# Block 0 of an attention-and-FFN kernel by halves of the heads, with four d_ff tiles begun early

## The chip, the cores and the metric

The kernel runs on 1 core of one Trainium2 chip. The metric is the device time of one execution in microseconds (us), lower is better. Its engines are TensorE (PE, with its weight loads shown apart as PEld), VectorE (DVE), ScalarE (ACT), GpSimd (POOL) and SyncE (SP), which here does nothing but issue transfers. Each engine works through its own instructions in order; semaphores tie them together.

## The reference, cut to what matters

```python
# q, k, v: (8, 8, 576, 64); w_in: (512, 2048); w_out: (2048, 512)
scores = 1/sqrt(64) * q_c @ k_c.T        # within chunks of 64 positions
attn = softmax(scores)
out = attn @ v_c                         # (8, 8, 576, 64)
x = out.transpose(0, 2, 1, 3).reshape(4608, 512)
h = maximum(x @ w_in, 0)
y = h*h @ w_out                          # (4608, 512), float32
```

Attention is local to chunks of 64 positions. Its result, with the 8 heads side by side in 512 columns, goes through a feed-forward network (FFN) with a squared ReLU.

## The kernel before, in words

**Tiling.** The 4608 tokens are 18 groups of 256, and two groups are a block of 512 tokens, so there are nine blocks. For each group the kernel loads q, k and v in fp32 and takes the upper halves of their words as bf16 (the index `1::2` after a bitcast). q and k are transposed so that the head's 64 elements lie on the partitions (`transpose_qk`, lines 414 to 428; from group 4 on by a cast on POOL and a transposing transfer on SP, `cast_q`, `cast_k`, `transpose_qk_dma`, lines 446 to 462). `scores` (464) makes all scores of a group in one PSUM bank pair of 128x1024 and ACT takes their exponential into `e`. `values` (496) multiplies by V, whose tiles hold a column of ones behind each head's 64, so that the sum of the exponentials comes out as column 65; `out_of_x` (438) takes its reciprocal on DVE (line 442) and multiplies (line 443) into `x`. `transpose_x` (530) or, in block 0, `transpose_x_early` (517) turns x into xT, the right operand of the FFN. `ffn_in` (573) makes h in 16 tiles of 128 d_ff rows (ft 0 to 15), each from four matmuls (dt 0 to 3, 128 of the 512 columns of x each: two heads each); ACT does the ReLU (590) and DVE or ACT the square (596, 598) into gT. `ffn_out_by_ft` (895) makes the output of block 0; blocks 1 to 8 use forms with fewer products (`ffn_out`, 728, and the quads from line 652 on).

**Heads and chunks.** On the 128 partitions lie two chunks. For the odd heads the chunks of a pair are swapped, so V of the even heads is kept in tiles `ve_sb` (two per group) and V of the odd heads in tiles `vo_sb` that start half a tile (64 positions) earlier; five `vo_sb` tiles serve the two groups of a block, the first and the last of them half full.

**Block 0 (lines 967 to 991).** The two groups follow each other. SP issues, in this order: q and k of group 0, q and k of group 1 (512 KB each, in runs of 512 B), nine V loads (128 KB or 64 KB each, in runs of 256 B), then the eight w_in loads (512 KB each, all 512 rows of 256 columns, runs of 1 KB). The first w_in load is cast half by POOL and half by ACT (lines 330 to 335). On PE stand: the transposes of q and k of group 0, of q of group 1, the scores of group 0, the transposes of k of group 1, then values, scores and x transposes of both groups, with `keep_busy` (430) matmuls of no use in the places where PE would wait. `ffn_in` of block 0 begins with ft 0 and 1 for the 256 tokens of group 0, then for those of group 1, then the other 14 tiles for all 512 tokens.

**What sets the order.** The order on each engine is that of the program (`manual_schedule`, line 205). From block 0's FFN on, a plan by slots places the attention of later blocks between FFN steps (lines 1004 to 1077): a slot is one step of `ffn_in` or `ffn_out`. In the plan of block 0 (`j == 0`) one load of group 4 or 5 (block 2) is issued in each of the first slots: first q and k, then V. In the plan of block 1 (`j == 1`) the casts of groups 4 and 5 stand in slots 16 and 20, their transposing transfers in slots 21 and 25, their scores in slots 36 and 37, and their values in 38 and 40. From its ninth load on SP waits, before it issues a load, for the landing of the one eight loads earlier: eight semaphores go round.

Of the kernel before, what the change touches and what calls it, by code (L numbers as in the profile page):

```python
# [144 lines left out]
def kernel(  # L145
# [9 lines left out]
    nc = tc.nc  # L155
# [83 lines left out]
    n_rec = itertools.count()  # L239
    v_even = [w_pool.tile([128, 2, n_hp, D + 1], FP32, name=f"ve_sb{i}") for i in range(NV)]  # L240
    v_odd = [w_pool.tile([128, n_hp, D + 1], FP32, name=f"vo_sb{i}") for i in range(NO)]
    for vt in v_even:
# [61 lines left out]
    def v_pieces(g):  # L304

        even, odd = [], []
        for t, p, m, b, s in runs(g):
            even.append(lambda t=t, p=p, m=m, b=b, s=s: nc.sync.dma_start(  # L308
                out=v_even[g % NV][p:p + m, t, :, 0:D],
                in_=v[b, 0::2, s:s + m, :].rearrange("h s d -> s h d")))  # L310
        for n, p, m, b, s in odd_loads[g]:
            odd.append(lambda n=n, p=p, m=m, b=b, s=s: nc.sync.dma_start(  # L312
                out=v_odd[n % NO][p:p + m, :, 0:D],
                in_=v[b, 1::2, s:s + m, :].rearrange("h s d -> s h d")))
        if g < 2:
            yield from [even[0], *odd[:-1], even[1], odd[-1]]
        else:
            yield from even + odd

    def go(pieces):  # L320
        for f in pieces:
            f()
# [3 lines left out]
    def load_w_in(i, n_cast=1):  # L326
# [4 lines left out]
        for c in range(0, 256, n):  # L331
            if i == 0 and c:
                return lambda: nc.scalar.copy(out=w_in_bf[:, :, c:c + n], in_=st[:, :, c:c + n])
            nc.gpsimd.tensor_copy(  # L334
                out=w_in_bf[:, :, i * 256 + c:i * 256 + c + n], in_=st[:, :, c:c + n])
# [180 lines left out]

    def transpose_x_early(g, t):
        psb = ps_ffn.tile([128, 512], FP32, name="ps_ffn").bitcast(BF16)
        x = state["x", g]
        for hp in range(n_hp):  # L520
            nc.tensor.transpose(
                out=psb[:, hp * 128:(hp + 1) * 128],
                in_=x[:, t, hp].rearrange("p a d -> p (a d)"),
                identity=ident)
        copy = nc.vector.tensor_copy if t and g else nc.scalar.copy
        copy(
            out=x_tile(g // 2)[:, g % 2 * 2 + t].rearrange("p h q -> p (h q)"),
            in_=psb[:, 0:512])

# [41 lines left out]
    FT_ORDER = [*range(n_ft // 2, n_ft), *range(n_ft // 2)]  # L571

    def ffn_in(j, parts):
        gT = gT_main.rearrange("p (u h) (f t) -> p u h f t", u=2, f=4)
        xT = xTs[j]
        for u, (c, n, ft) in enumerate((c, n, ft) for c, n, fts in parts for ft in fts):
            h = ps_ffn.tile([128, 512], FP32, name="ps_ffn")
            for dt in range(n_dt):
# [4 lines left out]
                    start=(dt == 0), stop=(dt == n_dt - 1))  # L583
            if n == 512 or u % 2 == 0:
                state["rl"] = state.get("rl", -1) + 1
                rl_tile = relu_sb[state["rl"] % 4]
                if j < 3:
                    rl_tile = rl_tile.bitcast(BF16)
            rl = rl_tile[:, u % 2 * 512:] if n < 512 else rl_tile
            nc.scalar.activation(out=rl[:, 0:n], in_=h[:, 0:n], func=AF.Relu)  # L590
            u0, u1 = c // GT, (c + n) // GT
            dst = gT[:, u0:u1, ft // 4, ft % 4, :]
            src = rl[:, 0:n].rearrange("p (u t) -> p u t", t=GT)
            if (n == 512 and ft in SQUARES_ON_ACT) or (
                    n < 512 and ft in (12, 3)) or (j == 0 and u == 0):
                nc.scalar.activation(out=dst, in_=src, func=AF.Square)
            else:
                nc.vector.tensor_tensor(out=dst, in0=src, in1=src, op=ALU.mult)  # L598
            yield

# [376 lines left out]
    keep_busy(6)  # L977
    AV(0, [1])
    transpose_x_early(0, 0)
    keep_busy(10)  # L980
    transpose_x_early(0, 1)
    AV(1, [0])
    AV(1, [1])
    keep_busy(4)
    transpose_x_early(1, 0)
    cast_first()
    keep_busy(8)
    transpose_x_early(1, 1)
    first_ffn_in = ffn_in(0, [(0, HT, (0, 1)), (HT, HT, (0, 1)), (0, BT, range(2, n_ft))])
    next(first_ffn_in)  # L990
    next(first_ffn_in)

    for i in range(1, 8):
        load_w_in(i, n_cast=2 if i < 5 else 1)
# [9 lines left out]
    for j in range(QUADS):  # L1004
# [6 lines left out]
        if j == 0:  # L1011
            loads, go_slots = pieces(far), range(17)
            at(28, summed(b11_p_b21, b11, b21))
# [6 lines left out]
        elif j == 1:  # L1020
# [201 lines left out]
```

## Time and profile before

| | us |
|---|---|
| median of 3 runs | 277.83 (276.78 to 278.43) |
| the profiled execution, its own time | 276.91 |
| its span from the first to the last instruction | 275.1 |
| PE busy in it | 264.9 (96%) |
| DVE, ACT, POOL busy | 199.2, 168.3, 89.6 |
| PE's first matmul of the FFN | starts at 17.46 |
| granted TensorE clock | 1.0 throughout |

Times in the profile are us from the start of the span. A timeline row gives start and length of a run of like instructions, engine, line, what is written from what, shape, count, and in brackets how long the engine sat idle before and what released it. The chain of waits is followed back from the last instruction. A view of stretches gives the busy time of each engine in each stretch, the granted clock, the mean busy share of the 16 DMA engines and the GB/s moved. "Landing" is the time from issue until all of a transfer's data has arrived.

### The profile page before, as it was taken

The page shows a single profiled execution, that of the slowest core. Times are in us where ns is not written, and L with a number is a line of the kernel's source. Part 1 is how long each engine was busy: PE and PEld are TensorE (multiplying, and loading weights), DVE is VectorE, ACT ScalarE, POOL GpSimd, SP SyncE. Part 2 cuts the span into 40 slices and gives each one's busy share as a digit, 9 for nine tenths or more (in the row PEclk, how much of TensorE's full clock was granted, in tenths as well). Part 3 has the DMA queues.
Part 4 walks back from the last instruction along what each step waited for, and adds up shares of the span by engine and source line. Part 5 has one row for each costly group of instructions (what it writes and reads, how often), then busy time and mean ns, then how long its engine had stood idle before and what let it go on. Part 6 is the DMA issues. An engine that isn't in the chain of part 4 may idle for free.

```text
span 275.1 us, 7923 instructions
## 1 busy us (share of the span) xinstructions
PE 264.9 (96%) x3261; PEld 203.4 (74%) x3261; DVE 199.2 (72%) x365; ACT 168.3 (61%) x300; POOL 89.6 (33%) x122
## 2 busy tenths in 40 slices
PE   2999999999999999999999999999999999999995
PEld 2764445888774588447878888888888888888884
DVE  1457514999538592499989998799779877994752
ACT  1657614894458883877678765565746665756430
POOL 2048834240360012040245224551643212331600
PEclk9999999999999999999999999999999999999999
DMA  7999999999999999999999999697999530220223
GB/s 216 262 352 389 361 332 270 339 213 172 262 210 218 238 234 218 275 223 178 228 236 197 218 238 194 103 220 196 244 187 224 123 76 2 99 55 7 71 83 114
DMA packets 136056, 55.60 MB, mean 202 GB/s; under 512 B 104273, under 2 KB 131921, under 8 KB 136017
## 3 DMA queue, kind: packets, MB, share of 16 engines
q1 hardware_dynamic: 133248, 46.54, 74.0%
q0 software_dynamic: 2624, 8.39, 9.6%
q8 instruction: 26, 0.43, 0.6%
q10 hardware_dynamic: 144, 0.13, 0.1%
q14 instruction: 14, 0.11, 0.1%
HBM read 36.70 MB, written 9.44 MB: 168 GB/s over the span
## 4 chain that ended last, share of the span: by engine, by line
PE 87%; DMA 4%; SPq 3%; DVE 3%; ACT 1%; issue 1%; ACTq 0%; DVEq 0%
PE ps_ffn L657 22%; PE ps_out L780 22%; PE ps_ffn L579 17%; PE ps_ffn L780 14%; PE ps_ffn L901 5%; PE ps_att L510 3%; PE ps_att L540 2%; DMA vo_sb<-in_v_dram 2%; PE ps_att L483 2%; DMA xT<-x 2%; DVE gT L598 2%; SPq L266 1%; SPq L308 1%; SPq L312 1%; DVE x L443 1%; ACT e L494 1%
## 5 line engine op out<-in xcount | busy, mean ns | idle before, releaser
L579 PE MATMUL ps_ffn<-xT,w_in_bf 128*128 128x512 bf16 (+1 forms) x328 | 57.8, 333 | 0.0
L780 PEld LDWEIGHTS <-w_st 128*128 128x128 bf16 x512 | 48.9, 98 | 6.6 <-DVE w_st L614 0.5
L665 DVE CUSTOM_DVE_ANT_0 relu<-ps_ffn,w_st 128x512 f32<-128x512 f32 x60 | 39.3, 684 | 13.0 <-PE ps_ffn L657 11.6
L579 PEld LDWEIGHTS <-w_in_bf 128*128 128x128 bf16 x328 | 31.2, 98 | 21.6 <-POOL w_in_bf L334 0.2
L598 DVE TENSOR_TENSOR gT<-relu 128x256 bf16<-128x256 bf16 (+2 forms) x68 | 34.1, 537 | 17.8 <-ACT relu L590 17.3
L590 ACT ACTIVATE relu<-ps_ffn 128x256 bf16<-128x256 f32 (+2 forms) x82 | 39.4, 501 | 9.4 <-PE ps_ffn L579 8.6
L657 PE MATMUL ps_ffn<-qk_st,w_in_bf 128*128 128x256 bf16 x240 | 35.3, 273 | 0.1
L657 PEld LDWEIGHTS <-w_in_bf 128*128 128x128 bf16 x320 | 30.7, 98 | 4.1 <-issue 0.3
L809 POOL DMA_DIRECT2D out_dram<-o_sb x24 | 17.6, 733 | 43.6 <-DVE o_sb L614 23.3
L780 PEld LDWEIGHTS <-gT 128*128 128x128 bf16 x296 | 28.6, 98 | 3.3
L780 PE MATMUL ps_out<-w_out_bf,w_st 128*128 128x256 bf16 x240 | 30.8, 273 | 0.0
L699 ACT ACTIVATE w_st<-ps_ffn 128x512 f32<-128x512 f32 x20 | 11.9, 597 | 29.6 <-PE ps_ffn L657 29.6
L443 DVE TENSOR_TENSOR x<-ps_att,recs 128x512 bf16<-128x512 f32 x36 | 24.9, 692 | 1.2
L657 PEld LDWEIGHTS <-qk_st 128*128 128x128 bf16 x240 | 22.6, 98 | 3.2 <-DVE qk_st L614 0.3
L657 PE MATMUL ps_ffn<-xT,qk_st 128*128 128x256 bf16 x160 | 23.9, 273 | 0.0
L676 POOL TENSOR_TENSOR qk_st<-relu 128x512 bf16<-128x512 f32 x10 | 10.3, 1034 | 41.6 <-DVE relu L665 38.1
L494 ACT ACTIVATE e<-ps_att 128x1024 bf16<-128x1024 f32 x18 | 18.3, 1025 | 8.5 <-PE ps_att L483 8.5
L676 POOL TENSOR_TENSOR gT<-relu 128x512 bf16<-128x512 f32 x10 | 10.3, 1033 | 35.4 <-DVE relu L665 30.5
L449 POOL CAST qkb<-qk_st 128x1024 bf16<-128x1024 f32 x12 | 13.0, 1082 | 14.9 <-DMA qk_st<-in_q_dram 14.9
L674 ACT ACTIVATE gT<-relu 128x512 bf16<-128x512 f32 x28 | 17.7, 631 | 0.0
L780 PE MATMUL ps_ffn<-w_out_bf,w_st 128*128 128x256 bf16 x144 | 17.7, 273 | 0.0
L614 DVE TENSOR_TENSOR w_st<-gT,w_st 128x1024 bf16<-128x1024 bf16 x26 | 16.8, 682 | 0.0
(92 smaller groups left out, 428.7 us busy)
## 6 DMA issues: line engine op xcount, KB each, us to landing
qk_st<-in_q_dram SPq DMA_DIRECT2D x16, 512.0 KB, 5.6
out_dram<-o_sb POOLq DMA_DIRECT2D x28, 256.0 KB, 3.9
qk_st<-in_k_dram SPq DMA_DIRECT2D x24, 256.0 KB, 5.6
ve_sb<-in_v_dram SPq DMA_DIRECT2D x32, 128.0 KB, 3.9
w_st<-in_moe_w_in_dram SPq DMA_DIRECT2D x8, 512.0 KB, 5.9
w_st<-in_moe_w_out_dram SPq DMA_DIRECT2D x8, 512.0 KB, 5.5
vo_sb<-in_v_dram SPq DMA_DIRECT2D x24, 128.0 KB, 3.6
qk_st<-in_k_dram SPq DMA_DIRECT2D x4, 512.0 KB, 5.8
```

Source lines behind the costliest of these rows:

```text
L443: nc.vector.tensor_tensor(out=x, in0=o[:, :, :, 0:D], in1=rec.to_broadcast([128, 2, n, D]), op=ALU.mult)
L494: nc.scalar.activation(out=e_out, in_=s_in, func=AF.Exp, scale=scale)
L579: nc.tensor.matmul(out=h[:, 0:n], lhsT=w_in_bf[:, dt, ft * 128:(ft + 1) * 128], rhs=xT[:, c // 128:(c + n) // 128, dt, :], start=(dt == 0) ...
L590: nc.scalar.activation(out=rl[:, 0:n], in_=h[:, 0:n], func=AF.Relu)
L598: nc.vector.tensor_tensor(out=dst, in0=src, in1=src, op=ALU.mult)
L614: nc.vector.tensor_tensor(out=out, in0=in0, in1=in1, op=op)
L657: nc.tensor.matmul(out=bank[:, f * GT:(f + 1) * GT], lhsT=a[:, dt, ft * 128:(ft + 1) * 128], rhs=b[:, :, dt, :], start=(first and f == 0 a ...
L665: nc.vector._custom_dve(TENSOR_ADD_SAT, out=out, in0=in0, in1=in1, s0=BIG, s1=0.0)
L674: engine.activation(out=dst, in_=r, func=AF.Square)
L676: engine.tensor_tensor(out=dst, in0=r, in1=r, op=ALU.mult)
L780: nc.tensor.matmul(out=out_ps, lhsT=lhsT, rhs=b[:, i, :], start=(first and i == 0 and (last or t == 0)), stop=(i == HF - 1), skip_group_ch ...
L809: dma.dma_start(out=out[t0:t0 + GT, col:col + HD].rearrange("(t p) d -> p t d", p=128), in_=o_sb.rearrange("p (t d) -> p t d", d=HD))
```

## The change

Block 0 is no longer worked group by group but by halves of the heads: heads 0 to 3 for all 512 tokens, then heads 4 to 7.

- Loads: q and k of a half are 512 KB each as before, now in runs of 1 KB (four rows of a head). V comes by single heads: for each half two loads of 128 KB (even heads) and two of 96 KB (odd heads) and two edges of 32 KB. To take them in one transfer, V tiles of block 0 lie in one tile (`ve_first`, `vo_mid`), which later blocks use in turn as before. w_in for ft 0 to 3 comes in four loads of 256 KB, by halves of the rows: dt 0 and 1 behind q and k of the second half, dt 2 and 3 behind V of the second half. SP's order: q, k, 6 V loads; q, k, 2 w_in, 6 V loads; 2 w_in; then w_in 2 to 7. All four are cast by POOL, none by ACT.
- Transposes of q and k: per half 16 matmuls each, and two copies out of each PSUM bank, one per pair of heads. q's two go to DVE; of k's, the first goes to ACT and the second to DVE. In the built program the DVE copy of k waits for the ACT copy of the same bank.
- Four d_ff tiles (ft 0 to 3, 512 tokens) are begun as soon as their operands exist: dt 0 and 1 (heads 0 to 3) around the scores and values of the second half, dt 2 after the x transposes of heads 4 and 5, dt 3 after those of heads 6 and 7. They stay open in four PSUM banks meanwhile. The squares of ft 0 to 3 all go to DVE in block 0.
- Fillers: 8 before the first scores, 8 after them, 4 before the last x transposes.
- Block 2: V of groups 4 and 5 is no longer issued in the plan of block 0; it is issued in the plan of block 1, slots 18 and 22, and the transposing transfers of q and k move to slots 16 and 20, right behind the casts. So on SP each group's transposing transfer stands ahead of its V loads, where before both stood behind all V loads.

```diff
+    v_first = w_pool.tile([128, 4, n_hp, D + 1], FP32, name="ve_first")
+    v_mid = w_pool.tile([128, 3, n_hp, D + 1], FP32, name="vo_mid")
...
+    def load_w_in_half(r):
+        st = w_st[next(n_staged) % 5].rearrange("p (a f) -> p a f", a=2)
+        for c in (0, 256):
+            nc.sync.dma_start(
+                out=st[:, :, c:c + 256],
+                in_=moe_w_in[256 * r:256 * r + 256, c:c + 256].rearrange("(a p) f -> p a f", p=128))
+            nc.gpsimd.tensor_copy(
+                out=w_in_bf[:, 2 * r:2 * r + 2, c:c + 256], in_=st[:, :, c:c + 256])
...
+        for hp in range(NH):
+            copy = nc.vector.tensor_copy if hp or not which else nc.scalar.copy
+            copy(out=qkT[:, which, hp].rearrange("c (p i) -> c p i", i=4),
+                 in_=psb[:, hp].rearrange("c i p -> c p i"))
...
+    def first_tile(ft, dts):
+        if dts[0] == 0:
+            first_h.append(ps_ffn.tile([128, 512], FP32, name="ps_ffn"))
+        for dt in dts:
+            nc.tensor.matmul(
+                out=first_h[ft],
+                lhsT=w_in_bf[:, dt, ft * 128:(ft + 1) * 128],
+                rhs=xTs[0][:, :, dt, :],
+                start=(dt == 0), stop=(dt == n_dt - 1), skip_group_check=True)
+
+    def first_in():
+        for ft in range(4):
+            first_tile(ft, (3,))
+            squared(0, ft, first_h[ft], 0, BT, ft)
+            yield
+        yield from ffn_in(0, [(0, BT, range(4, n_ft))])
...
-    HT = BT // 2
-    go(pieces([0, 1]))
-    cast_first = load_w_in(0, n_cast=2)
-    TE(0)
-    transpose_qk(1, ps_ffn, None)
-    SC(0)
-    transpose_qk(1, None, ps_ffn)
-    keep_busy(8)
-    AV(0, [0])
-    SC(1)
...
+    act = nc.scalar.copy
+    for half in range(2):
+        qk_half, v_half = half_loads(half)
+        go(qk_half)
+        if half:
+            load_w_in_half(0)
+        go(v_half)
+    load_w_in_half(1)
+    transpose_half(0, 0, ffn_bank())
+    transpose_half(0, 1, ffn_bank())
+    keep_busy(8)
+    scores_half(0)
     keep_busy(8)
-    transpose_x_early(1, 1)
...
+    values_half(0, 0)
+    values_half(0, 1)
+    transpose_half(1, 0, ffn_bank())
+    transpose_x_half(0, 0, ffn_bank(), act)
+    transpose_x_half(0, 1, ffn_bank(), act)
+    transpose_half(1, 1, ffn_bank())
+    scores_half(1)
+    first_tile(0, (0, 1))
+    first_tile(1, (0, 1))
+    values_half(1, 0)
+    first_tile(2, (0, 1))
+    values_half(1, 1)
+    first_tile(3, (0, 1))
+    both = att_bank()
+    transpose_x_half(1, 0, both[:, 0:256], act)
+    for ft in range(4):
+        first_tile(ft, (2,))
+    both = att_bank()
+    fill(4, both[:, 256:384])
+    transpose_x_half(1, 1, both[:, 0:256], nc.vector.tensor_copy)
+    first_ffn_in = first_in()
...
-            loads, go_slots = pieces(far), range(17)
+            loads, go_slots = itertools.chain(*map(qk_pieces, far)), range(17)
...
-                for slot, f in ((16 + 4 * i, C), (21 + 4 * i, TD), (36 + i, SC), (38 + 2 * i, AV),
+                for slot, f in ((16 + 4 * i, C), (16 + 4 * i, TD), (36 + i, SC), (38 + 2 * i, AV),
                                 (41 + 2 * i, XT)):
                     at(slot, f, g)
+                at(18 + 4 * i, lambda g=g: go(v_pieces(g)))
```

`transpose_half`, `scores_half`, `values_half` and `transpose_x_half` do for half of the heads and 512 tokens what `transpose_qk`, `scores`, `values` and `transpose_x_early` do for all heads and 256 tokens; each has as many matmuls and as large a result as the old one.

More of the change, by code (lines that the diff above doesn't have):

```diff
@@ L526, in transpose_x_early, with fill @@
[L526 to L528 removed]
+        copy(out=x_tile(0)[:, :, NH * half + hp, :], in_=psb.rearrange("p (t q) -> p t q", t=4))
+    def fill(n, out):
+        for _ in range(n):
+            nc.tensor.matmul(out=out, lhsT=ident, rhs=ident, start=True, stop=True)
     def transpose_x(g):
```

156 lines of the change are left out of this document (111 added, 45 removed).

## The prediction

> **What bounds the kernel now.** I read the busy totals and slices of the page first, then PE's waits, then the chain of waits, then the timeline of the first 32 us.
>
> ```profile
> PE 264.9 (96%) x3261; PEld 203.4 (74%) x3261; DVE 199.2 (72%) x365; ACT 168.3 (61%) x300; POOL 89.6 (33%) x122
> ...
> PE   2999999999999999999999999999999999999995
> ```
>
> ```profile
> PE ps_ffn L400 <- DMA qk_st<-in_q_dram: 5.2, 2, 4.8
> PE ps_ffn L400 <- DMA qk_st<-in_k_dram: 0.4, 1, 0.4
> PE ps_ffn L657 <- DVE qk_st L614: 0.2, 1, 0.2
> ```
>
> ```profile
> 10.73 4.93 DMA vo_sb<-in_v_dram
> 17.46 14.01 PE ps_ffn L579 x72
> 31.47 7.77 PE ps_ffn L901 x36
> ```
>
> PE is busy for 264.9 of 275.1 us, and its one long wait is the 4.8 us for the first q. After that it is the bound. So what happens ahead of 31.47, the end of block 0's first FFN stage, moves the end of the kernel by as much; what happens beside PE later moves nothing unless PE has to wait. A matmul of 512 columns takes 7.77/36 = 0.216 us. The stage's own work, 56 of these and 16 of half the width, is 64 x 0.216 = 13.8 of its 14.01 us. Ahead of it the chain names the last V load, issued at 10.73 and landed 4.93 later, at 15.66.
>
> ```profile
> 4.77 1.06 PE L400 MATMUL ps_ffn<-ident,qk_st 128*64 128x128 bf16 x16 [4.77 <-DMA qk_st<-in_q_dram]
> 6.26 1.06 PE L400 MATMUL ps_ffn<-ident,qk_st 128*64 128x128 bf16 x16 [0.42 <-DMA qk_st<-in_k_dram]
> 7.37 1.07 ACT L409 COPY qkT<-ps_ffn 128x512 bf16<-128x512 bf16 x2 [5.34 <-PE ps_ffn L400]
> 8.74 0.64 PE L483 MATMUL ps_att<-qkT 64*64 64x64 bf16 x32
> 8.86 1.29 DVE L409 COPY qkT<-ps_ffn 128x512 bf16<-128x512 bf16 x2 [1.69 <-PE ps_ffn L400]
> 9.44 1.02 ACT L494 ACTIVATE e<-ps_att 128x1024 bf16<-128x1024 f32 x1 [1.00 <-PE ps_att L483]
> 10.36 1.03 PE L433 MATMUL ps_ffn<-ident 128*128 128x128 bf16 x8
> 12.83 0.22 PE L510 MATMUL ps_att<-ve_sb,e 64*64 64x65 bf16 x2 [0.19 <-DVE x L443]
> 13.23 0.21 DVE L442 RECIPROCAL recs<-ps_att 128x8 f32<-128x8 f32 x1 [0.46 <-PE ps_att L510]
> 13.48 0.69 DVE L443 TENSOR_TENSOR x<-ps_att,recs 128x512 bf16<-128x512 f32 x1
> 14.22 0.40 PE L521 MATMUL ps_ffn<-ident,x 128*128 128x128 bf16 x4 [0.18 <-DVE x L443]
> 14.66 0.58 ACT L526 COPY xT<-ps_ffn 128x512 bf16<-128x512 bf16 x1 [0.55 <-PE ps_ffn L521]
> 16.43 0.61 PE L433 MATMUL ps_ffn<-ident 128*128 128x128 bf16 x8
> 16.79 0.61 POOL L334 CAST w_in_bf<-w_st 128x512 bf16<-128x512 f32 x1 [14.59 <-DMA w_st<-in_moe_w_in_dram]
> 17.48 0.42 DVE L526 COPY xT<-ps_ffn 128x512 bf16<-128x512 bf16 x1 [0.49 <-PE ps_ffn L521]
> 18.11 1.17 POOL L334 CAST w_in_bf<-w_st 128x512 bf16<-128x512 f32 x2 [0.70 <-DMA w_st<-in_moe_w_in_dram]
> 19.46 2.67 POOL L334 CAST w_in_bf<-w_st 128x512 bf16<-128x512 f32 x4 [0.18 <-DMA w_st<-in_moe_w_in_dram]
> ```
>
> These rows are the price list: a k load waited for to the first copy 1.11 (6.26 to 7.37); a copy out of PSUM 0.535 on ACT, 0.645 on DVE; scores to exponential 0.70 (8.74 to 9.44), exponential 1.02; values to reciprocal 0.40, to product 0.65, product 0.69; x transposes to copy 0.44, that copy 0.58 on ACT, 0.42 on DVE. An engine starts about 0.05 after what released it.
>
> **The change part by part.** *Loads.* The order changes, the bytes up to dt 2 and 3 of ft 0 to 3 do not: 2 MB of q and k, 1 MB of V, 1 MB of w_in, which before had landed at 18.11.
>
> ```profile
> 3.00:9.25 6.25, 3.63 (x80) 2.98 (x80) 1.68 (x3) 1.07 (x2) 0.00 (x0) 1.00 1.16 341
> 9.25:14.00 4.75, 4.56 (x120) 3.66 (x108) 2.52 (x6) 3.60 (x5) 0.00 (x0) 1.00 1.33 227
> 14.00:27.00 13.00, 12.41 (x110) 7.10 (x110) 8.50 (x16) 8.73 (x18) 8.41 (x12) 1.00 1.07 373
> ```
>
> In the last column q and k in runs of 512 B move at 341 GB/s, V in runs of 256 B at 227, w_in in runs of 1 KB at 373. A q or k load took 1.49 us (4.77 to 6.26), a w_in load 1.32 and 1.35 (16.79, 18.11, 19.46), so runs of 1 KB should save q and k 0.14 each, bounded by nothing and 0.17. The first k then lands at 5.98, and the last early weights at 18.11 - 4 x 0.14 = 17.55, cast by 18.16. V's loads of 64 and 128 KB overlapped at 227 GB/s, 0.58 us per 128 KB, so I count the new ones by bytes too; the other end is the second rival below. [...]
>
> *Attention.* Per half there is the same number of matmuls, so the question is latency. From the first k at 5.98: ACT's copy starts 7.09 and ends 7.63; DVE's copy of the same bank waits for it and ends 8.33; the second half of the scores runs at 8.38 and the exponential from 8.8 to 9.82. Values at 9.87, reciprocal 10.3 (0.40, and I take 0.43 while PE is slow), x of heads 0, 1 ready 11.25, of heads 2, 3 at 12.2, since DVE makes them one behind the other. Then x transposes, ACT's copies to 13.27; PE reaches the second k at 12.5, behind the x transposes: its bytes end at 5.98 + 2.3 for half of V + 2 x 1.35 = 11.0, at 12.8 with all of V's old lag (first rival), and I take 12. ACT copies its first part from 13.32 to 13.86, DVE the second to 14.55 (DVE's q copies, 1.29, end at 13.5 and stay hidden). Scores, exponential 14.95 to 15.97, values 16.02, x of heads 4, 5 ready 17.35, its transposes 17.40, ACT's copy to 18.42. Four dt 2 matmuls, 0.86, to 19.33; the 4 fillers, at most 0.3, to 19.55; x of heads 6, 7 is ready since 18.3 but stands behind these; transposes, DVE's copy to 20.41, dt 3 at 20.46.
>
> *FFN.* Left from there are 4 + 48 matmuls: 52 x 0.216 = 11.22, so the stage ends at 31.68 and not at 31.47: **0.2 us later**. The 12 matmuls moved ahead lie in waits and cost nothing, but they save only 2.6 us, while the half-by-half chain has two exponentials and four x products one behind the other and starts its last matmuls 3 us later than the old stage began. The weights (18.16) and the last V (17.55 less a w_in load of 1.33, so 16.2, needed at 16.9) are hidden by 0.3 and 0.7 us: if transfers are later by more than that, they are next. The removed ACT cast and ACT square, and the square moved to DVE, cost nothing:
>
> ```profile
> 22.92 5.16 DVE L598 TENSOR_TENSOR gT<-relu 128x512 bf16<-128x512 bf16 x6 [1.26 <-ACT relu L590]
> ```
>
> a square is 0.86 on DVE, a tile on PE 4 x 0.216 = 0.86, so DVE keeps pace, and 14 of them from 21.7 end at 33.8, when the output stage still uses the first tiles. Were that cover gone, one square is 0.86.
>
> *Block 2.* Here only slack is bought.
>
> ```profile
> 61.66 6.17 SPq L460 DMA_TRANSPOSE qkT<-qkb  x2
> ...
> 68.80 0.45 PE L483 MATMUL ps_att<-qkT 64*64 64x64 bf16 x32
> ...
> 70.15 0.44 PE L483 MATMUL ps_att<-qkT 64*64 64x64 bf16 x32
> ...
> 73.93 0.22 PE L510 MATMUL ps_att<-ve_sb,e 64*64 64x65 bf16 x2
> ```
>
> ```profile
> DMA to landing us min/median/max: 4.9/5.5/6.2
> ```
>
> ```profile
> 58.86 1.17 POOL L454 CAST qkb<-qk_st 128x1024 bf16<-128x1024 f32 x1 [1.61 <-DMA qk_st<-in_k_dram]
> ```
>
> The second transposing transfer, issued about 64.75, lands 4.9 later at 69.7; its scores run at 70.15 without a wait, 0.45 us of slack. After, it waits on SP for the cast that ends at 60.03 and behind group 4's five V loads, about 61.8, and lands some 3 us earlier; behind it on SP stand group 5's V, out by about 67 and, by the same 4.9, landed by 72, needed at 73.93. So 0; without it only a gain in block 0 beyond 0.45 us would be lost here. If V came 3 us later than I say, PE would wait 1 us.
>
> *Sum.* 276.91 + 0.2 = 277.1 against the profiled execution, which lies 0.92 below the median of 277.83; against that median 278.0.
>
> **Rivals.** *Transfers set the end, as before, and they come early (faster).* V's 1 MB at 227 GB/s should end 4.6 us after 9.25, at 13.9; it landed at 15.66. If that lag of 1.8 us does not come back, early weights are cast at 16.4 and V is there at 14.4. By transfers alone dt 2 would then end at 17.3 and, with fillers, transposes and the last copy, dt 3 start at 18.4: the stage ends at 29.6, 1.85 us earlier, 276.0. That takes a copy chain 2 us shorter than mine. For it: PE's share of the chain is priced partly at its slow early pace, and may rise sooner. Against it: the copies, exponentials and products on the chain are DVE's and ACT's, whose durations the rows fix.
>
> *Loads in flight are too few (slower).* From the ninth load on each waits for the landing of the eighth before it, and now 20 loads stand up to the early weights where 15 stood.
>
> ```profile
> DMA to landing us min/median/max: 5.1/5.8/9.4
> ```
>
> This is the w_in and w_out loads' landing. Eight per 5.8 us is 0.73 each: load 8 at about 8.4 (5.98 and half of V) plus 12 x 0.73 = 17.2, no loss against 17.55. At 7.6, midway to the 9.4 seen, it is 0.95 each: 19.8, cast 20.4, dt 2 to 20.9, fillers, last x copy, dt 3 at 22.1: 1.6 us beyond my sum, so 279.6. It begins to cost from about 6.2 us per landing.
>
> *PE falls back to its slow pace in the waits.* Eight fillers took 1.03 us at 10.36 and 0.61 at 16.43: PE is slow at first, though the granted clock reads 1.00 throughout. If the waits between 14.9 and 20.4 bring this back, and it lasts from 8.74 to about 11.5 again, 2.8 us run at half pace: 1.4 us, so 279.4. Against it: waits of 0.5 to 1.5 us in 12 to 17 did not do so. [...]
>
> *It does not do what it says:* the first tiles wait for each other and the 12 early matmuls run in the end anyway: 2.6 us less hidden, 280.6.
>
> **How the numbers follow.** My forecast (276.9 to 279.0 from the 1 KB bound, the start-up pace and the difference of two medians) gets 0.68; the faster rival 0.16, of which I put 0.11 beyond 0.5%, since a chain shortened by half as much gives 277; few in flight 0.09, slow pace 0.04, no overlap 0.03. 0.5% is 1.4 us, about what a measurement of this kernel tells from no change. So faster 0.12 (0.11 and a tail of the forecast), slower 0.14 (the last three less a little), same 0.74. The range takes in most of the faster rival and the slow pace: 276.2 to 279.4.
>
> **What would show it.** In the profile after: FFN matmuls without a break from about 20.5, ending about 31.7; DVE copies of k behind ACT's; the last fillers ahead of the last x transposes although x is ready; casts of early weights done by 18.2; the scores of group 5 with no wait. Wrong if the unbroken FFN starts before 19.3 or after 21.6, or if PE waits for V, a cast or a transposing transfer.

## The result, and the profile after

The kernel after takes **279.78 us** in the median of 22 runs (277.99 to 282.93), the kernel before 278.09 in 22 runs beside it (276.78 to 280.04). The ratio of their runs is **1.0068**, with a 95% interval of 1.0047 to 1.0088: about 1.9 us slower (1.3 to 2.4). The forecast was 278.0 with a range of 276.2 to 279.4, no change beyond 0.5%; it was too low, and the time lies just above its range.

The profiled execution of after took 282.04 us (span 280.2), near the slow end of its own spread, so what is seen only there has to be told from what every execution shows. First the page: busy time, the PE and DMA rows of the 40 slices, and the first two rows on the chain that ended last.

```profile
PE 263.7 (94%) x3234; PEld 200.8 (72%) x3237; DVE 202.3 (72%) x367; ACT 165.8 (59%) x293; POOL 92.0 (33%) x123
...
PE   3779999999899899999999999999999999999994
...
PE 66%; DMA 15%; DVE 8%; SPq 6%; ACT 2%; issue 2%; POOL 1%; DVEq 0%; ACTq 0%; POOLq 0%
PE ps_ffn L781 18%; PE ps_out L904 18%; PE ps_ffn L904 11%; PE ps_ffn L699 8%; DMA qkT<-qkb 7%; PE ps_ffn L1025 5%; DVE gT L692 4%; DMA qk_st<-in_k_dram 4%; DMA vo_sb<-in_v_dram 2%; PE ps_att L509 2%; DMA w_st<-in_moe_w_in_dram 2%; SPq L459
```

PE is as busy as before in us and stands more: the last work is now followed back through transfers for 15% of the span (4% in before), and the transposing transfers of q and k (qkT<-qkb) alone have 7%. The waits of PE, in the view of waits, say where (us in total, times, longest):

```profile
PE ps_att L482 <- DMA qkT<-qkb: 2.6, 3, 1.3
...
PE ps_ffn L622 <- DVE x L442: 0.7, 2, 0.4
PE ps_att L588 <- ACT qkT L575: 0.7, 1, 0.7
PE ps_ffn L713 <- ACT xT L626: 0.7, 1, 0.7
...
PE ps_ffn L713 <- DVE xT L626: 0.5, 1, 0.5
PE ps_ffn L713 <- POOL w_in_bf L556: 0.5, 1, 0.5
```

Now block 0 of after in the timeline of PE, from the scores of the second half on:

```profile
13.88 0.32 PE L588 MATMUL ps_att<-qkT 64*64 64x64 bf16 x16 [0.68 <-ACT qkT L575]
14.60 0.32 PE L588 MATMUL ps_att<-qkT 64*64 64x64 bf16 x16 [0.41 <-DVE qkT L575]
...
17.54 0.39 PE L622 MATMUL ps_att<-ident,x 128*128 128x128 bf16 x4
18.60 0.59 PE L713 MATMUL ps_ffn<-xT,w_in_bf 128*128 128x512 bf16 x2 [0.67 <-ACT xT L626]
19.65 0.60 PE L713 MATMUL ps_ffn<-xT,w_in_bf 128*128 128x512 bf16 x2 [0.45 <-POOL w_in_bf L556]
20.31 0.39 PE L622 MATMUL ps_att<-ident,x 128*128 128x128 bf16 x4
21.22 1.02 PE L713 MATMUL ps_ffn<-xT,w_in_bf 128*128 128x512 bf16 x4 [0.52 <-DVE xT L626]
22.28 1.02 PE L699 MATMUL ps_ffn<-xT,w_in_bf 128*128 128x512 bf16 x4
```

Up to 17.54 this is the forecast within 0.2 us, the DVE copy of k behind ACT's included. Then dt 2 of ft 2 and 3 waits for its weights (19.65), and the last x transposes, held back by it, come at 20.31. dt 3, from which the forecast counted its unbroken FFN (20.46), starts at 21.22, still inside the 21.6 that it gave as its limit; the other twelve tiles, called the long run below, start at 22.28. Of the forecast's signs of being wrong, PE's waits for a cast and for transposing transfers are here. Block 0's output stage starts at 32.63 in after, and at 31.30 in before (after's row, then before's):

```profile
32.63 1.24 PE L1025 MATMUL ps_ffn<-w_out_bf,gT 128*128 128x512 bf16 x4
```

```profile
30.22 1.24 PE L579 MATMUL ps_ffn<-xT,w_in_bf 128*128 128x512 bf16 x5
31.30 1.46 PE L901 MATMUL ps_ffn<-w_out_bf,gT 128*128 128x512 bf16 x6
```

So block 0 cost 1.33 us in this execution. Two waits for transposing transfers follow, at 72.74 for group 5 and at 93.52 for group 7. The steps there, from the start of PE's matmul before the wait to the start of the one behind it, are 1.55 and 1.52 us:

```profile
70.53 0.93 PE L904 MATMUL ps_ffn<-w_out_sum,w_st 128*128 128x256 bf16 x7
72.74 0.45 PE L482 MATMUL ps_att<-qkT 64*64 64x64 bf16 x32 [1.28 <-DMA qkT<-qkb]
```

With the 2.6 us of these waits (a third is short), block 0 makes 3.9 of the 5.1 us between the two profiled spans. But the medians are only 1.7 us apart. Which of this does the change cost always, and which did one execution add?

### The profile page after: what moved, and what is told of

It is laid out like the page before. It is cut to its first block, busy times and chain, and to the rows that moved or that the text cites. A ratio compares the mean times of both kernels' runs of the same rounds, so it can differ in the third digit from the quotient of the medians.

```text
span 280.2 us, 7877 instructions
## 1 busy us (share of the span) xinstructions
PE 263.7 (94%) x3234; PEld 200.8 (72%) x3237; DVE 202.3 (72%) x367; ACT 165.8 (59%) x293; POOL 92.0 (33%) x123
## 4 chain that ended last, share of the span: by engine, by line
PE 66%; DMA 15%; DVE 8%; SPq 6%; ACT 2%; issue 2%; POOL 1%; DVEq 0%; ACTq 0%; POOLq 0%
PE ps_ffn L781 18%; PE ps_out L904 18%; PE ps_ffn L904 11%; PE ps_ffn L699 8%; DMA qkT<-qkb 7%; PE ps_ffn L1025 5%; DVE gT L692 4%; DMA qk_st<-in_k_dram 4%; DMA vo_sb<-in_v_dram 2%; PE ps_att L509 2%; DMA w_st<-in_moe_w_in_dram 2%; SPq L459 2%; PE ps_att L482 1%; SPq L312 1%; PE ps_att L642 1%
## 5 line engine op out<-in xcount | busy, mean ns | idle before, releaser
L699 PE MATMUL ps_ffn<-xT,w_in_bf 128*128 128x512 bf16 (+1 forms) x304 | 54.4, 334 | 0.0
L692 DVE TENSOR_TENSOR gT<-relu 128x512 bf16<-128x512 bf16 (+2 forms) x68 | 36.0, 570 | 15.6 <-ACT relu L685 15.4
L685 ACT ACTIVATE relu<-ps_ffn 128x512 bf16<-128x512 f32 (+2 forms) x80 | 39.0, 512 | 12.4 <-PE ps_ffn L699 8.0
L699 PEld LDWEIGHTS <-w_in_bf 128*128 128x128 bf16 x304 | 28.9, 98 | 20.8 <-issue 0.3
L781 PEld LDWEIGHTS <-w_in_bf 128*128 128x128 bf16 x320 | 30.7, 98 | 4.5 <-issue 0.7
L493 ACT ACTIVATE e<-ps_att 128x1024 bf16<-128x1024 f32 x16 | 16.3, 1025 | 8.4 <-PE ps_att L482 8.3
L448 POOL CAST qkb<-qk_st 128x1024 bf16<-128x1024 f32 x12 | 13.8, 1147 | 22.6 <-DMA qk_st<-in_q_dram 17.7
```

The costliest lines, as they stand in the source:

```text
L493: nc.scalar.activation(out=e_out, in_=s_in, func=AF.Exp, scale=scale)
L699: nc.tensor.matmul(out=h[:, 0:n], lhsT=w_in_bf[:, dt, ft * 128:(ft + 1) * 128], rhs=xT[:, c // 128:(c + n) // 128, dt, :], start=(dt == 0) ...
L781: nc.tensor.matmul(out=bank[:, f * GT:(f + 1) * GT], lhsT=a[:, dt, ft * 128:(ft + 1) * 128], rhs=b[:, :, dt, :], start=(first and f == 0 a ...
```

## The experiments

Ratios are to the kernel before, run beside each; in brackets the 95% interval. Every profile is of one execution. After itself stands at 1.0068.

**Each part alone.** Block 0 alone, with block 2 in its old order (e1), and block 2 alone, with the old block 0 (e2). The edit of e1 undoes what e2's makes:

```diff
-            loads, go_slots = itertools.chain(*map(qk_pieces, far)), range(17)
+            loads, go_slots = pieces(far), range(17)
...
-                for slot, f in ((16 + 4 * i, C), (16 + 4 * i, TD), (36 + i, SC), (38 + 2 * i, AV),
+                for slot, f in ((16 + 4 * i, C), (21 + 4 * i, TD), (36 + i, SC), (38 + 2 * i, AV),
...
-                at(18 + 4 * i, lambda g=g: go(v_pieces(g)))
```

> The kernel after with the order of block 2 as it was before (V of groups 4 and 5 in the plan of block 0, transposing transfers behind them). Theory A: block 0 costs 1.3 us (early weights cast at 19.6 instead of 18.2, first FFN matmul of the long run at 22.3) and sends the whole load stream out 3.5 us later, so that with the old order group 5's transposing transfer lands some 3 us later than the 69.7 of before and its scores wait about 3 us: no faster than after, 280 to 282. Rival B: the new order of block 2 is itself what makes the transposing transfers late (after: scores of group 5 start 1.55 us late at 72.74, those of group 7 1.52 us late at 93.52): this kernel then loses both waits and comes to 278.0 to 278.5.

> The kernel before with the new order of block 2 alone; block 0 as before. Theory A: loads of groups 4 and 5 land as in before, the second transposing transfer lands ahead of 69, no wait appears, time within 0.4 us of before. Rival B: the order itself delays the transfers behind group 4's V and the cast: group 5's scores wait about 1.5 us and the time is 1 to 1.5 us over before.

e1: 1.0059 [1.0026, 1.0092], 280.33 us. e2: 1.0019 [0.9981, 1.0057], 279.2 us. The loss comes with block 0; the new order alone is not told from none. Rival B falls. Theory A does not fare well either: e1's profile has no wait for group 5's transposing transfer, and no wait for a weight (rows of PE's timeline in e1):

```profile
18.79 1.02 PE L713 MATMUL ps_ffn<-xT,w_in_bf 128*128 128x512 bf16 x4 [0.67 <-ACT xT L626]
19.87 0.39 PE L622 MATMUL ps_att<-ident,x 128*128 128x128 bf16 x4
20.78 1.02 PE L713 MATMUL ps_ffn<-xT,w_in_bf 128*128 128x512 bf16 x4 [0.52 <-DVE xT L626]
21.84 1.46 PE L699 MATMUL ps_ffn<-xT,w_in_bf 128*128 128x512 bf16 x6
```

The four dt 2 run in one piece, and still the output stage starts at 32.2, 0.9 later than in before. In e2 the second transposing transfer goes out at 63.50, 1.3 us earlier than in before (64.80) and not 3.

**Early weights.** In e3 each half comes in one load of 512 KB, not two of 256 KB; in e5 ACT issues the two loads for dt 2 and 3 behind its first copy.

```diff
+        nc.sync.dma_start(
+            out=st,
+            in_=moe_w_in[256 * r:256 * r + 256, 0:512].rearrange("(a p) f -> p a f", p=128))
         for c in (0, 256):
-            nc.sync.dma_start(
-                out=st[:, :, c:c + 256],
-                in_=moe_w_in[256 * r:256 * r + 256, c:c + 256].rearrange("(a p) f -> p a f", p=128))
```

```diff
-    load_w_in_half(1)
     transpose_half(0, 0, ffn_bank())
     transpose_half(0, 1, ffn_bank())
+    load_w_in_half(1, nc.scalar)
```

> The kernel after with each pair of 256 KB early weight loads made one of 512 KB (18 loads up to the early weights and not 20; all else the same). Theory A (eight loads in flight, each new one waiting for the landing of the eighth before it, let the queues run dry from 14 to 18 us): the last early load is issued near 12.8 and not 14.4, is cast by about 18.8, the last x transposes come 0.6 to 0.8 us earlier, time 0.5 to 1.0 us below after. Rival C (the chain of copies, exponentials and x products sets the end; weights hide): no change within 0.3 us.

> The kernel after with the two loads of the early weights for dt 2 and 3 issued by ACT behind its first copy (about 7.1 us) and no longer by SP at the end of the line. Theory A: they land by about 14, dt 2 of ft 2 and 3 waits for nothing, the run of FFN matmuls begins 0.6 to 0.8 us earlier, and w_in 2 to 7 go out 1 to 2 us earlier, so later transfers too: 0.7 to 2 us below after. Against it: V of the second half lands later than the 15.2 of after by 512 KB at 227 to 373 GB/s, 1.4 to 2.3 us, and is needed at 16.05, so the gain can be eaten up to 1.4 us. Rival C: no gain in any case, since the chain of copies sets the end, and a loss of 0.5 to 1.4 by V.

e3: 1.0041 [1.0009, 1.0072]; e5: 1.0070 [1.0030, 1.0110]. What e3 gains over after lies within the intervals. In e5 all four casts are done by 15.3, and still the long run starts at 22.01 and the output stage at 32.4. So theory A's block 0 falls: the weights' lateness was real in after's profile, but with it gone the stage is nearly as late. Theory C, the chain, stays.

**The chain of copies.** e6 gives each of k's two copies a bank of its own, so that DVE does not wait for ACT (in after 0.69 us until 7.69 and 0.49 until 13.86). e7 puts the x transposes of heads 6 and 7 ahead of dt 2 and drops the four fillers.

```diff
-    transpose_half(0, 1, ffn_bank())
+    transpose_half(0, 1, (ffn_bank(), ffn_bank()))
...
-    transpose_half(1, 1, ffn_bank())
+    transpose_half(1, 1, (ffn_bank(), ffn_bank()))
```

```diff
+    both = att_bank()
+    transpose_x_half(1, 1, both[:, 0:256], nc.vector.tensor_copy)
     for ft in range(4):
         first_tile(ft, (2,))
-    both = att_bank()
-    fill(4, both[:, 256:384])
-    transpose_x_half(1, 1, both[:, 0:256], nc.vector.tensor_copy)
```

> The kernel after with the transposes of k written to two PSUM banks per half, one for each pair of heads, so that DVE's copy need not wait for ACT's. Theory D (the chain of copies, exponentials and x products sets the start of the long run of FFN matmuls, 0.3 to 0.5 us later than forecast, and weights only add to it in some runs): the chain is 0.5 to 0.6 us shorter in each half, the long run starts near 21.2 instead of 21.8 to 22.3, time 0.5 to 1.2 us below after. Theory A (early weights set it, cast at 19.6): the long run starts within 0.2 us of where it did, no change in time.

> The kernel after with the x transposes of heads 6 and 7 ahead of the four dt 2 matmuls and without the four fillers. Theory D: DVE's last copy (0.7 us) and the transposes lie beside ACT's copy and dt 2, so dt 3 follows dt 2 without a wait, the long run starts 0.9 to 1.1 us earlier, about 20.9 to 21.3, and the time is 0.9 us below after. Theory A: dt 2 of ft 2 and 3 waits for its weights as before, and only the part behind it (fillers, transposes, copy: 20.09 to 21.22 in after) goes: also near 1 us, but with a wait for the weights of 0.5 or more in front of dt 2.

e6: the long run at 21.21, as theory D has it, but 1.0069 [1.0035, 1.0103]: no gain in time. Its profile, of an execution of 282.24 us, has 4.0 us of waits for transposing transfers. e7: long run at 21.38, and **1.0208** [1.0152, 1.0263], 283.43 us, 4 us slower than after. What happened is at the other end of the program. PE's timeline and the stretches of e7 (us, then busy time of PE, PEld, DVE, ACT, POOL, granted clock, DMA share, GB/s):

```profile
250.00 0.49 PE L781 MATMUL ps_ffn<-xT,qk_st 128*128 128x256 bf16 x3
252.77 0.28 PE L781 MATMUL ps_ffn<-xT,qk_st 128*128 128x256 bf16 x1 [2.28 <-issue]
```

```profile
250.00:255.00 5.00, 2.72 (x17) 1.87 (x15) 0.69 (x1) 1.48 (x3) 1.00 (x1) 0.81 0.05 13
255.00:260.00 5.00, 5.00 (x41) 4.20 (x39) 2.77 (x4) 2.27 (x5) 0.03 (x1) 0.85 0.00 0
```

PE stands 2.28 us for nothing that the profile shows, and gets 0.81 and 0.85 of the clock in these stretches. The DMA view of 249 to 251.5 us in e7 holds instruction fetches and nothing else:

```profile
DMA packets 5, 0.05 MB, mean 20 GB/s; under 512 B 0, under 2 KB 0, under 8 KB 0
...
q14 instruction: 4, 0.03, 4.6%
q8 instruction: 1, 0.02, 3.3%
```

Dropping the fillers makes PE's program eight instructions shorter, four matmuls and four weight loads; that this shifts what a fetch brings in time is a guess. (Before has the same five fetches in that stretch and PE does not stand, so their number is not it.) To test whether the length matters, e12 has e7's order but puts the four fillers behind the first scores, so the length is after's:

```diff
     scores_half(0)
-    keep_busy(8)
+    keep_busy(12)
```

> The run with the x transposes of heads 6 and 7 ahead of dt 2 lost 2.3 us of PE at 250 us, where four 8 KB and one 16 KB instruction fetches came at the same moment. Here the same edit with the four fillers put behind the first scores and not left out, so PE's instructions are as many as in after and its fetches fall as in after. If the place of the fetches made the stall: no stall near 250, long run of FFN matmuls from about 21.0, time 278.5 to 279.5, 3 to 5 us below the run without fillers. Rival (the earlier copies or the shorter block 0 disturb the end in another way): 282 to 284 again.

e12: 1.0049 [1.0027, 1.0071], 279.36 us: 4 us come back, and PE's idle time near 250 is 0.39 us. So the stall came with leaving the four fillers out and not with the order of block 0; whether PE lacked a fetch, and which, is not shown. And the earlier x transposes do what theory D said: the long run starts at 20.56, the output stage at 30.9. e8, with the edits of e5, e6 and e7 at once, lacks the fillers too and has the same stall (2.23 us, again with nothing that releases it):

> The kernel after with three edits: two banks for k, x transposes of heads 6 and 7 ahead of dt 2 without fillers, and the early weights of dt 2 and 3 issued by ACT behind its first copy. Theory D: gains add, the long run starts near 20.0, block 0's output stage 2 us earlier than in after and about 1 us earlier than in before, time 277.0 to 277.8. Theory A: the ACT issue matters most; without its effect on later transfers the sum would be the same, so this run tells only whether block 0 can be made shorter than before's. If the part over before that is left in after (some 0.5 to 1 us) comes from waits for transposing transfers in blocks 2 and 3, it stays: 278.0 to 278.5.

e8: 1.0223 [1.0173, 1.0272]. It decides nothing on block 0 beyond that PE waited 0.90 us for V with ACT issuing weights.

**Waits for transposing transfers.** e9 has the scores of groups 5 and 7 three slots later. e10 (on after) and e11 (on before) make the scores of each odd group from 5 on out of the even group's transposed q and k, which leaves the odd groups' attention wrong and every transfer in place.

```diff
-                for slot, f in ((16 + 4 * i, C), (16 + 4 * i, TD), (36 + i, SC), (38 + 2 * i, AV),
+                for slot, f in ((16 + 4 * i, C), (16 + 4 * i, TD), (36 + 3 * i, SC), (38 + 3 * i, AV),
...
-                slots = {SC: (6, 10), AV: (12, 22)
+                slots = {SC: (6, 13), AV: (12, 22)
```

```diff
         qkT = state.pop(("qkT", g))
+        if g >= FIRST_DMA_T:
+            qkT = state["pair"] = state["pair"] if g % 2 else qkT
```

> The kernel after with the scores of groups 5 and 7 (the two that waited for their transposing transfers in after's profile, 1.5 us each) three slots later, 39 for 37 and 13 for 10, and the values of group 5 one slot later. Theory E (block 0 costs about 1 us in every run, and the rest of the loss and its spread come from these two waits, which only some runs have): median 0.5 to 1.5 us below after, highest run below 281. Rival: the spread has other causes: no change.

> The kernel after, where the scores of each odd group from 5 on are made from the transposed q and k of the even group before it, so they never wait for their own transposing transfer; all transfers stay, the attention of the odd groups is left wrong. Theory F (block 0 costs 0.9 to 1.3 us in every run and waits of PE for transposing transfers in blocks 2 and 3 make the rest of the difference and most of the spread from run to run): 278.3 to 279.2, with runs closer together. Rival (block 0 alone costs it all): no change from after, ratio to before again 1.007.

> The kernel before with the same edit (scores of odd groups from 5 on made from the even group's transposed q and k; their attention left wrong). Theory F: before had 0.45 us of slack there and waits in few runs, so 0 to 0.5 us below before. What lies between this run and the one on the kernel after is then block 0 by itself, 0.9 to 1.3 us. Rival: as far below before as that one is below after.

e9: 1.0125 [1.0087, 1.0162]; its profile has new steps, 1.03 at 77 us in group 5's values, 0.83 at 96, 1.13 at 126. e10: 1.0127 [1.0079, 1.0174], from only six runs (278.98 to 283.79); e11: 1.0013 [0.9990, 1.0037]. Theories E and F fall: taking the two waits away shows no gain. (e9's profile also has PE at half its clock in block 0, 0.50 from 16 to 17, taken up below under PE's slow pace.) The second profile of after (e17) says why.

> The kernel after unchanged, for a second profile beside the other three on one chip. Theory: in a run with another landing of loads the waits of 1.5 us for the transposing transfers of groups 5 and 7 are not there or elsewhere (other kernels of the same block 0 showed none), block 0 is 0.7 to 1.3 us later than in before in any case, and x waits for DVE by 0.5 to 1.3 us near 56 or 124 us. Rival: the same two waits of 1.5 us at the same places again, as a fixed cost of the change. Time 279.3 to 280.3 by both.

e17 is after unchanged: 1.0072 [1.0046, 1.0097], 280.08 us; its profiled span is 277.6. No wait for a transposing transfer of groups 5 and 7 is left in it, but the second half starts late (PE's timeline in e17, and then the same lines in after):

```profile
10.60 1.07 PE L569 MATMUL ps_ffn<-ident,qk_st 128*64 128x128 bf16 x16
...
12.90 1.06 PE L569 MATMUL ps_ffn<-ident,qk_st 128*64 128x128 bf16 x16
...
19.37 1.02 PE L713 MATMUL ps_ffn<-xT,w_in_bf 128*128 128x512 bf16 x4 [0.67 <-ACT xT L626]
20.45 0.39 PE L622 MATMUL ps_att<-ident,x 128*128 128x128 bf16 x4
21.35 1.02 PE L713 MATMUL ps_ffn<-xT,w_in_bf 128*128 128x512 bf16 x4 [0.52 <-DVE xT L626]
22.41 0.81 PE L699 MATMUL ps_ffn<-xT,w_in_bf 128*128 128x512 bf16 x3
```

```profile
10.51 0.64 PE L569 MATMUL ps_ffn<-ident,qk_st 128*64 128x128 bf16 x16
...
12.56 0.64 PE L569 MATMUL ps_ffn<-ident,qk_st 128*64 128x128 bf16 x16
```

Sixteen transposes take 1.06 us in e17 and 0.64 in after: PE is still in its slow pace beyond 13.9 us. It costs dt 2 some 0.8 us (19.37 for 18.60). The profiles of e3 and e7 are slow for as long, those of e1, e6, e9 and e10 fast from 8.3 to 10.6 on. e17's output stage starts at 32.8, 1.5 later than before's, and its span ends 2.4 later. Most of the rest is one step at 125 us, where PE waits 0.85 for x (e17, then before):

```profile
120.67 3.56 DVE L692 TENSOR_TENSOR gT<-relu 128x512 bf16<-128x512 f32 x3
...
125.13 0.62 PE L642 MATMUL ps_att<-ident,x 128*128 128x128 bf16 x8 [0.85 <-DVE x L442]
...
120.80 1.45 POOL L448 CAST qkb<-qk_st 128x1024 bf16<-128x1024 f32 x1 [8.71 <-DMA qk_st<-in_q_dram]
```

```profile
119.20 2.86 DVE L598 TENSOR_TENSOR gT<-relu 128x512 bf16<-128x512 f32 x3
...
118.44 1.03 POOL L449 CAST qkb<-qk_st 128x1024 bf16<-128x1024 f32 x1 [7.83 <-DMA qk_st<-in_q_dram]
```

POOL's casts start when their loads land; here the later load puts two of them (1.45 and 1.24 us) beside the three squares that DVE must do ahead of x, where before has one (1.30, at 120.21), and the squares take 3.56 for 2.86. Three squares with no cast beside them take 1.89 (before, at 123.66), a cast with little beside it 1.03. The same wait stands in e10 and e12, where the three squares take 3.56 too. That it is the casts was read from such rows, not isolated by a run.

**A short block 0.** e13 joins e6's two banks, e12's order and e3's weight loads. e14 is e13 with block 2 in its old order (e1's edit). e15 and e16 are e13 and e14 with the second weight load issued by ACT behind the first exponential (edit against e13):

```diff
-    load_w_in_half(1)
...
     scores_half(0)
+    load_w_in_half(1, nc.scalar)
     keep_busy(12)
```

> The kernel after with all that shortened block 0: two banks for k, x transposes of heads 6 and 7 ahead of dt 2 with the four fillers moved behind the first scores, early weights in two loads of 512 KB. Theory D: long run from about 20.3, block 0's output stage at about 30.8, 0.5 us earlier than in before. Theory F: the gain over after turns partly into longer waits for transposing transfers, as in the run with two banks for k (1.5, 0.9, 1.6 and 1.2 us of waits there): 278.0 to 279.5. If F is wrong and block 0 alone decides: 277.0 to 277.6.

> The kernel with the short block 0 (two banks for k, x transposes ahead of dt 2, fillers moved, early weights in two loads) and the order of block 2 as it was before. If the new order of block 2 costs some 0.5 us by itself, as the run of that part alone hints (1.002 of before, not certain): 277.5 to 278.2, level with before. If the new order is free and later waits come from the load stream alone: 278.5 to 279, as with the new order, with waits for transposing transfers of group 5 of 1 us or more, since V stands ahead of them again.

> The short block 0 with the early weights of dt 2 and 3 (one load of 512 KB) issued by ACT behind its first exponential, at about 10 us, and not by SP behind V at 12.8 to 14.4. If the DMA queues running dry from 14 to 18 us is what makes later loads and transposing transfers late: no dry stretch, group 5's transposing transfer in time, 0.5 to 1 us below the same kernel without it (278.7), 277.7 to 278.2. If not: no change, 278.4 to 279.

> Both: the short block 0, weights issued by ACT behind the first exponential, block 2 in its old order. If each is worth 0.5 us this is the fastest, 277.0 to 277.7, at or under before. If neither matters: 278.5 to 279.

| run | output stage of block 0 from | span profiled | median | ratio | runs at a mean granted clock of 0.994 or less |
|---|---|---|---|---|---|
| e13 | 30.7 | 276.6 | 278.74 | 1.0022 [0.9999, 1.0045] | 0 of 12 |
| e14 | 30.7 | 277.0 | 278.60 | 0.9997 [0.9970, 1.0024] | 2 of 12 |
| e15 | 33.4 | 277.3 | 279.41 | 1.0036 [1.0006, 1.0066] | 10 of 12 |
| e16 | 34.3 | 278.8 | 279.00 | 1.0024 [0.9995, 1.0052] | 9 of 12 |

With block 0 1.9 us shorter than in after's profile, the loss is gone within the interval (e14), or nearly (e13). With block 2 in its old order the pair is e1 with the long block 0, 1.0059, and e14 with the short one, 0.9997, and their intervals do not overlap: there the long block 0, its chain and its weight loads, is the cause. But its end alone does not set the time. In e6, e12 and e18, with the new order, the output stage starts at 31.6, 30.9 and 30.9, near or ahead of before's 31.30, and yet they stand at 1.0069, 1.0049 and 1.0049. What else they lose is open. And no kernel beats before in the median, though block 0 is done 0.6 us earlier in e13 and e14. In e14 the next limit takes it: PE waits for group 5's transposing transfer and for x at 124 (step 1.18):

```profile
71.04 0.45 PE L482 MATMUL ps_att<-qkT 64*64 64x64 bf16 x32 [1.55 <-DMA qkT<-qkb]
```

And e15 has V 1.8 us late, since ACT's weight load went ahead of it, has block 0 done 2.7 us later than e13, yet its span is only 0.7 longer, without such a wait. The stretch in which the DMA engines ran short of work is gone in it (a DMA share of 1.08 to 1.19 from 14 to 18 us, 0.50 and 0.75 in after), but the time that was expected of that, 277.7 to 278.2, did not come. Part of the 2.7 us is PE's clock. The granted clock is 0.50 from 20 to 22 us, and dt 2 and 3 take 3.38 us there, 2.02 in e13 (a row of PE's timeline in e15, and two of its stretches, with columns as in e7's):

```profile
19.81 3.38 PE L714 MATMUL ps_ffn<-xT,w_in_bf 128*128 128x512 bf16 x8
...
20.00:21.00 1.00, 1.00 (x4) 0.30 (x2) 0.42 (x1) 0.00 (x0) 0.85 (x2) 0.50 1.08 380
21.00:22.00 1.00, 1.00 (x4) 0.36 (x3) 0.00 (x0) 0.00 (x0) 0.84 (x3) 0.50 1.07 365
```

The last column of the table shows how common this is: e15's profile has one such stretch, some 3.4 us long, and a mean clock of 0.994. The five runs of e15 and e16 without one took 276.70 to 277.77 us, all below before's median; the other 19 took 278.07 to 281.96. So weights that come early by ACT may be worth about 1 us in executions without such a stretch; five runs picked by their clock suggest it and do not show it. For after the clock is no main part of the loss: without the 4 of its 22 runs that have such a mean its median is 279.6. In e13 and e14, what is gained in block 0 beyond before's end is mostly waited for later.

Last, e18 moves three slots of e13 to take its waits away, and e19 moves one of them in before:

```diff
-                slots = {SC: (2, 2), AV: (6, 10), XT: (13, 15)}
+                slots = {SC: (2, 2), AV: (6, 8), XT: (13, 15)}
```

e18 has besides `(36 + 2 * i, SC)` for `(36 + i, SC)` and `SC: (6, 11)` for `SC: (6, 10)`.

> The short block 0 with the new order of block 2, and three slots of the plan moved: scores of groups 5 and 7 one slot later (38 for 37, 11 for 10), values of group 9 two slots earlier (8 for 10). Theory G (what block 0 costs passes through to the end; where block 0 is made shorter, waits for transposing transfers at groups 5 and 7 and a wait for x of group 9 behind DVE squares that POOL's casts slow down take the gain): these waits go, 276.9 to 277.9, at or under before. Rival: the loss stays or moves on to the next group, 278.4 to 279.

> The kernel before with the values of group 9 two slots earlier alone (8 for 10). In before's profile PE waits 0.27 us beyond its step for x of that group, 0.5 to 1.2 in the kernels with the new block 0. Theory G: 0.2 to 0.4 us below before, and the step near 122 us runs without a wait. Rival: no change; then the same slot is worth at most 0.2 in the new kernels too.

e18: 1.0049 [1.0020, 1.0077]; e19: 1.0030 [0.9996, 1.0064]. Theory G's remedy falls: in both, the earlier values now wait themselves, two waits for x of 0.5 us each near 120. But e19's profile, with the old block 0 and the old order, settles the transposing transfers:

```profile
69.99 0.45 PE L483 MATMUL ps_att<-qkT 64*64 64x64 bf16 x32 [1.19 <-DMA qkT<-qkb]
...
72.46 0.45 PE L483 MATMUL ps_att<-qkT 64*64 64x64 bf16 x32 [1.04 <-DMA qkT<-qkb]
```

e19's edit acts only near 120, so the kernel before has these waits too, in some executions. They are part of the spread of both kernels and no fixed cost of the change.

## Why the prediction was wrong, point by point

The step that failed is the sum of the FFN stage, "so the stage ends at 31.68 and not at 31.47: 0.2 us later". In the five profiles with after's block 0 the output stage started at 32.0 (e10), 32.2 (e1), 32.6 (after), 32.8 (e17) and 33.1 (e9), against 31.30 (31.1 to 31.4 in the four profiles with the old block 0): **0.7 to 1.8 us later**, about 1.2 in the mean. Its terms:

- *An end was compared with a start, 0.17.* 52 x 0.216 counts from start to start, so 31.68 is the start of the next stage, whose row in before is 31.30. The working itself meant 0.38.
- *A bank, 0.20, left out.* Four open tiles hold all four PSUM banks of the FFN, so the fifth tile waits for the first ReLU (21.63 to 22.23 in after, where the fifth tile starts at 22.28). From the first dt 3 to the fifth tile it is 1.06 in all five profiles (20.78 to 21.84 in e1, 21.35 to 22.41 in e17), not 4 x 0.216 = 0.86.
- *The chain itself, 0.1 to 0.3.* dt 3 was to start at 20.46; it starts at 20.58 in e10 and 20.78 in e1, where the first k landed 0.2 later. Copies one behind the other, exponentials, products and the last x transposes behind the fillers are as worked out.
- *PE's slow pace, 0.8 in some executions.* In e17, e3 and e7 PE has not yet become fast at 13.9; the working did not have this, and its "waits of 0.5 to 1.5 us in 12 to 17 did not do so" argued from a PE that was already fast: four x transposes took 0.40 at 13.09 and 14.22 in before, and 0.61 at 12.36 in e17.
- *PE's fall back to half its clock, 1.1 in e9.* This is the rival to which the forecast gave 1.4 us and a chance of 0.04. e9 has after's block 0; its granted clock is about half from 15 to 18.5, and dt 2 starts at 19.71, against 18.59 in e10 (stretches of e9, columns as in e7's):

```profile
15.00:16.00 1.00, 1.00 (x4) 0.21 (x2) 0.00 (x0) 0.88 (x1) 0.00 (x0) 0.55 0.97 250
16.00:17.00 1.00, 1.00 (x18) 0.43 (x18) 0.22 (x2) 0.00 (x0) 0.00 (x0) 0.50 0.71 180
```

The fall came although PE stood at most 0.68 us at a time from 11.7 to 15.1 (until 13.76, for ACT's copy of k). Runs of after and e17 with a mean clock of 0.994 or less are 7 of 34, so the chance was too low, if the stretch lies in block 0 in those too, which is not shown.

- *Early weights "hidden by 0.3".* Not in after, where the cast ended at 19.59 and not 18.16, and dt 2 waited 0.45; 0.40 in e6; hidden in e1, e10 and e17. The rival of eight loads in flight has its time nearly right (279.6) and its mechanism in the trace (in after SP stands 0.3 us ahead of its eighteenth load, until 11.99, for the landing of its tenth), but e3 and e5 show that it is not what sets the median.
- *Attention and V*: right, V was never late in after.
- *Block 2, 0:* right in time as far as e2 can tell, wrong in the working: "lands some 3 us earlier" is 1.3 in e2, since group 4's cast ends only at 56.66 and its transposing transfer and V loads, which stand ahead, go out up to 62.96; and in after, with all loads later, it goes out at 66.41, 1.6 later than in before.
- *That a gain beyond 0.45 us would be lost there*: seen in e14's profile, a wait of 1.55, and in part in e13's, two waits of 0.9 together.

What block 0 costs passes on to the end in these profiles. Their spans are longer than before's by a further 0.2 (e1), 1.4 (e10) and 1.0 us (e17), mostly by waits for x that come and go with the landing of loads; their share in the median stays open, and so does whether the order of block 2 adds up to 0.3%, since the intervals of e13 and e14 overlap.

## What to carry to other kernels

When two schedules are compared by a sum, compare start with start, and count the PSUM banks that open tiles hold (0.20 us here). The stage that is a chain of waits had a second price here, paid by chance: PE stayed in its slow pace for longer (sixteen transposes in 1.06 us and not 0.64, e17), or its granted clock fell to 0.50 (e9, e15), so look at the granted clock of every run. And a stage made shorter helps only up to the slack of the transfers behind it, so look for that slack first.

## What the runs showed of the hardware that was not expected

- Four fillers fewer on PE, eight instructions, cost 4 us (e7 against e12): amid instruction fetches PE stood 2.28 us at 250, and its granted clock was 0.81 and then 0.85 in the two stretches of 5 us from there. With the fillers back elsewhere it stood 0.39. e8, as short, stood 2.23 at a granted clock of 1.00.
- The same kernel left PE's slow pace anywhere from before 10.5 (after) to beyond 13.9 us (e17), over 3 us apart, while the granted clock read 1.00: sixteen transposes take 0.64 us at 10.51 in after, and 1.06 at 12.90 in e17. What sets the moment is not shown.
- The clock fell to half without a long idle stretch: in e9 PE was busy for 1.90 of the 3.41 us before 15.1 (for 1.88 in after, whose clock was 1.00 there and up to 26) and stood at most 0.68 at a time, and then its granted clock was about half for 3.4 us (0.50 from 16 to 17). In e15 and e16 the fall follows waits for V of 1.79 and 1.85 us; the clock is 0.50 from 20 to 22 in e15.
